# Attention steps in four rounds instead of three, fenced loads, and one expert piece a round before the gate

## The chip, the cores and the metric

The kernel runs on one core of a Trainium2 chip, as one program. Its time is the device time of that core in microseconds (us): the median of several executions. TensorE (PE) does the matrix products, VectorE (DVE), ScalarE (ACT) and GpSimd (POOL) work on the elements, SyncE (SP) issues nearly all the loads and stores. Each engine goes through its own list of instructions in the order in which the program was written; an instruction waits until its operands are there and its buffer is free, and all that stands behind it on that engine waits with it.

## The reference

Banded attention over 4 batches, 8 heads, 576 positions and 64 columns a head, then a mixture of 4 experts over the 2304 rows that come out:

```python
scores = q @ k.T / 8                           # per head, 576 x 576
mask   = rel in [0, 32)                        # heads 0 to 3
         rel in [0, 128) and rel % 4 == 0      # heads 4 to 7
attn   = softmax(where(mask, scores, -1e9))
x      = (attn @ v) as (2304, 512)
p      = probs / (probs.sum(-1) + 1e-9)        # (2304, 4)
out    = sum over e of p[:, e] * (relu(x @ w1[e]) @ w2[e])    # 512 -> 1024 -> 512
```

## The kernel before

**Attention.** The positions of heads 4 to 7 are sorted by their remainder by 4, so that every head has a plain band of 32 positions. A *group* is one batch, one pair of heads and a third (192) of the positions; a *step* is two groups, and there are 24 steps. A step goes through eight stages: `s_qk` (48 small products into two PSUM banks, tiles `sc`), `s_max` (DVE adds the mask and takes the smallest value of the negated scores: `sm`, `nm`), `s_sub` (POOL), `s_exp` (ACT), `s_sum` (DVE: sum, plus 1e-9, reciprocal), `s_norm` (POOL), `s_tr` (PE transposes into one bank, tile `pt`, ACT copies it to `pts`) and `s_av` (PE: 48 small products with `v` into two banks, tiles `po`, ACT copies them into the rows of x, tile `xr`). The pool `pa` of these banks has four, handed out in turn.

**Rounds.** The main loop (L746) runs over rounds `n`. In a round each stage is issued for the step that is `lag` rounds old, in the order of the table `stages` (L374): scores, maximum, subtraction and exponential of the newest step, sum and normalization of the one before, the transpose of the one two rounds back, `s_av` of the one three back. After step 4 and after step 9 three rounds start no step (`GAP`), so that the first positions of a batch are finished before the next are begun. All loads are issued by SP from `load_scores` and `load_values`, ahead of the stages and in one queue with the weights (`fetch_w1`, `fetch_w2`).

**Experts.** Each expert is cut into 4 *units* of 256 hidden columns: 16 units, each gone through twice (first for the 768 rows of block 0, then for blocks 1 and 2). Every fp32 operand is split into a high and a low part (ACT writes the high one, DVE or POOL the low one), and a product is three products of parts. x @ w1 of a unit is done with seven half-size products and sums of operands (Strassen-like): `x_sums` (L206, DVE) makes the sums of x in place, in tile `xr`, four a call; `x_part` (L218) splits one; `w1_split`, `w1_sums`, `w1_late` do the same for w1. Unit 0 of block 0 uses eight plain products instead (`plain`). The generator `experts` (L516 ff.) yields after each *piece*: 6 products of 384 columns (m1x, m1y) or one row tile of the second layer (6 products of 512 columns, tile `m`, which DVE adds to `acc`). A later visit of a unit has 13 pieces.

**How the two are interleaved.** Before round START (7) the rounds hold attention alone and dummy products (`dummies`, tile `wt`). From START on a round also takes pieces, 2 until round OPEN (15), where the *gate* opens, and `PACE` (10) from there on. Before the gate there are 7 pieces to do, the first half of unit 0; when they are done a round gets 6 dummies instead. With each piece `step()` runs one stage of a queue of splits and sums. After the last round, `gate` gets "over", and from the next time that a visit calls `begin()` the attention's pools are closed, larger ones are opened, and the parts of x of block 2 (`x_part` 4 and 5, `x_sums` 4 and 5) are queued. In the visit of unit 14 `need(x_sums, 5)` runs whatever of them is left at once.

The change touches the stage table, the eps addition in `s_sum`, the loads, the counts of pieces and dummies, and where unit 1's weights are split.

Of the kernel before, what the change touches and what calls it, by code (L numbers as in the profile page):

```python
# [21 lines left out]
PACE = 10  # L22
LAG = 3
# [3 lines left out]
FILL = 6  # L27
# [23 lines left out]
def kernel(  # L51
# [34 lines left out]
    ident = const.tile([128, 128], F32, name="ident")  # L86
    pw = const.tile([128, NTT, E], F32, name="pw")
# [39 lines left out]
    def w1_split(u):  # L127

        r = raw1[u]
        gh = wp.tile([128, 3, 2, 128], F32R, tag="g1h", name="g1h", bufs=2)  # L130
        gl = wp.tile([128, 3, 2, 128], F32R, tag="g1l", name="g1l", bufs=2)
        a11, a12 = r[:, 0:2, 0:128], r[:, 2:4, 0:128]
        a21, a22 = r[:, 0:2, 128:256], r[:, 2:4, 128:256]
        for i, a in enumerate((a11, a12, a22)):
            split(gh[:, i], gl[:, i], a, nc.scalar, nc.gpsimd if u > 1 else nc.vector)
            a_op[u, ("A11", "A12", "A22")[i]] = (gh[:, i], gl[:, i])
            yield
        if u == 0:
            gh, gl = (wp.tile([128, 4, FU], F32R, tag=t, name=t) for t in ("g2h", "g2l"))
            v = (slice(None), slice(0, 2), slice(128, 256))  # L140
            split(gh[v], gl[v], a21, nc.scalar, nc.vector)
            a_op[u, "A21"] = (gh[v], gl[v])
# [16 lines left out]
    def w1_late(u):  # L159
        r = raw1.pop(u)  # L160
        gh = wp.tile([128, 4, FU], F32R, tag="g2h", name="g2h")
        gl = wp.tile([128, 4, FU], F32R, tag="g2l", name="g2l")
        for n, c, f in (("S2", 0, 0), ("S1", 2, 128), ("S3", 0, 128), ("S4", 2, 0)):
            v = (slice(None), slice(c, c + 2), slice(f, f + 128))
            split(gh[v], gl[v], r[v], nc.scalar, nc.gpsimd if u > 1 else nc.vector)
            a_op[u, n] = (gh[v], gl[v])
            yield
        if u + 2 <= LAST:
            fetch_w1(u + 2)
# [59 lines left out]
    def attention(ap, xrp, pa):  # L229
# [78 lines left out]
        def s_sum(n, gs):  # L308
# [4 lines left out]
            nc.vector.tensor_scalar(  # L313
                out=su, in0=su, scalar1=1e-9, scalar2=None, op0=ALU.add
# [59 lines left out]
        stages = (  # L374
            (s_qk, 0), (s_av, 3), (s_tr, 2), (s_max, 0), (s_sum, 1), (s_sub, 0),
            (s_norm, 1), (s_exp, 0),
        )
        return chunk, load_masks, load_qk, load_v, stages
# [124 lines left out]
    def experts(begin):  # L503

        for half in range(2):
# [5 lines left out]
            if half == 1:  # L511
# [5 lines left out]
                prepare(w1_late, 1, soon=True)  # L517
# [76 lines left out]
    with tc.manual_schedule():  # L594
        make_identity(nc, ident)
        warm = ident.bitcast(mybir.dt.bfloat16)
# [30 lines left out]
        def done(*gs):  # L627

            return LAG + max(at(n) for n, s in enumerate(steps) if any(g in s for g in gs))

# [4 lines left out]
        def at(n):  # L635

            return n + GAP * sum(n > last for last in needed)

# [106 lines left out]
        first = 2 * (needed[0] + 1)  # L745
        dummies(18)  # L746
        ffn = experts(begin)
        for n in range(at(len(steps) - 1) + LAG + 1):
            load_scores(first if n <= needed[0] else len(flat))
            load_values(min(n + 1, qk_done // 2 + 3))  # L750
            for stage, lag in stages:
                m = step_at.get(n - lag)
                if m is not None:
                    stage(m, steps[m])
            if n in step_at:
                qk_done += 2
            av_done += n - LAG in step_at
# [17 lines left out]
            if n == 6:  # L775
                fetch_w1(1)
            if n == START:
                weigh(shares)
            if n == START + 1:
                prepare(w1_split, 1)  # L780
                prepare(w1_sums, 1)
            if n == OPEN - 1:
                prepare(w2_late, 1)
            if n == START + 2:
                fetch_w2(1)
            if n == OPEN:
                fetch_w1(2)
            if n == OPEN:
                gate.add("open")
            if n < START:  # L790
                dummies(FILL if n in step_at else FILL // 2)
# [5 lines left out]
            for _ in range(PACE if "open" in gate else 2):  # L797
                if next(ffn) == "idle":
                    dummies(FILL)
                    for _ in range(3):  # L800
                        step()
                    break
# [66 lines left out]
```

## Time and profile before

| | |
|---|---|
| median of 3 runs | 866.12 us (863.88 to 866.41) |
| the profiled execution | 863.98 us, of which the span of the trace is 862.2 us |
| PE busy | 825.6 us (96%), 6214 products |
| PE weight loads (PEld) | 730.6 us (85%) |
| DVE, ACT, POOL busy | 497.5 (58%), 320.4 (37%), 391.1 us (45%) |
| DMA | 59.18 MB, mean 69 GB/s |

Busy times are unions of the instructions' durations; products overlap one another in the array, so a PE busy to 100% is not the same in every stretch. "Idle before, releaser" in a row is the time in which the engine stood still before that instruction, and what ended it. PEclk is the share of the full TensorE clock that was granted (1.00 is 2.4 GHz, 0.50 is 1.2 GHz, values between them are means). The first 64 us are the rounds before the gate, then rounds and pieces run together until about 310 us, and the rest is experts alone.

### The profile page before, as it was taken

Reading aid. Unit: us, or ns where it says so; the run is one execution under the profiler, and the core shown is the slowest. Engines: PE = TensorE matmul, PEld = TensorE weight load, DVE = VectorE, ACT = ScalarE, POOL = GpSimd, SP = SyncE. Lnnn points to the kernel's source line nnn. Section 1 sums busy time; section 2 is a strip of 40 time slices with the busy share of each in tenths; the row PEclk is TensorE's granted clock in tenths of the full one; section 3 lists DMA queues with packets and bytes.
Section 4 is the critical chain, followed back from the end, with each engine's and each line's share of the span. In section 5 each row is a group of like instructions: output and inputs, shape, how many; then the busy total and the mean of one; then the engine's idle time right before and its main releaser. Section 6 shows DMA issues by size and latency. Waiting matters only on the chain.

```text
span 862.2 us, 15616 instructions
## 1 busy us (share of the span) xinstructions
PE 825.6 (96%) x6214; PEld 730.6 (85%) x6214; DVE 497.5 (58%) x1051; ACT 320.4 (37%) x759; POOL 391.1 (45%) x466
## 2 busy tenths in 40 slices
PE   7788999999989997899999999999999999999998
PEld 5657888889878896888989989899898898998986
DVE  4586667656865558655555555555545555555454
ACT  2454445445553444532422323333233242232321
POOL 3252768867767668633413422431432342342210
PEclk9899999999999999899999999999999999999999
DMA  7952323443422121301010010100100101000003
GB/s 218 232 142 92 107 85 97 127 138 101 126 69 75 67 74 50 123 24 49 25 49 25 27 49 25 49 25 25 50 25 24 49 25 48 26 25 25 0 24 123
DMA packets 49172, 59.18 MB, mean 69 GB/s; under 512 B 3641, under 2 KB 38585, under 8 KB 49099
## 3 DMA queue, kind: packets, MB, share of 16 engines
q1 hardware_dynamic: 48379, 57.53, 21.6%
q8 instruction: 49, 0.80, 0.4%
q10 hardware_dynamic: 720, 0.66, 0.2%
q14 instruction: 24, 0.20, 0.1%
HBM read 53.45 MB, written 4.72 MB: 67 GB/s over the span
## 4 chain that ended last, share of the span: by engine, by line
PE 86%; DVE 6%; DMA 2%; ACT 2%; POOL 1%; issue 1%; SPq 1%; ACTq 0%; DVEq 0%; POOLq 0%
PE m L483 44%; PE m1x L385 22%; PE m1y L385 17%; DVE xr L212 1%; PE po L352 1%; PE pt L332 1%; DMA v_s<-vw 1%; DVE acc L491 1%; PE sc L271 1%; DMA r<-w 1%; DVE sm L285 1%; SPq L256 1%; DVE xl_B L125 1%; DVE hl L409 1%; DVE xl_T L125 1%
## 5 line engine op out<-in xcount | busy, mean ns | idle before, releaser
L491 DVE SCALAR_TENSOR_TENSOR acc<-m,pn,acc 128x512 f32<-128x512 f32 x270 | 201.9, 749 | 136.3 <-PE m L483 135.9
L483 PE MATMUL m<-w2h,hh 128*128 128x512 f32 x576 | 228.0, 396 | 4.3 <-ACT hh L403 3.9
L483 PE MATMUL m<-w2l,hh 128*128 128x512 f32 x576 | 226.4, 393 | 0.0
L125 POOL TENSOR_TENSOR g2l<-r,g2h 128x256 fp32r<-128x256 f32 x120 | 88.7, 767 | 239.8 <-PE m L483 213.4
L483 PE MATMUL m<-w2h,hl 128*128 128x512 f32 x576 | 179.3, 393 | 0.0
L403 ACT ACTIVATE hh<-s 128x384 fp32r<-128x384 f32 x94 | 49.4, 526 | 248.0 <-DVE s L426 189.8
L483 PEld LDWEIGHTS m<-w2h,hh 128*128 128x128 f32 x576 | 108.8, 189 | 26.4 <-ACT hh L403 4.8
L483 PEld LDWEIGHTS m<-w2h,hl 128*128 128x128 f32 x576 | 108.7, 189 | 23.9
L483 PEld LDWEIGHTS m<-w2l,hh 128*128 128x128 f32 x576 | 108.9, 189 | 20.1
L125 POOL TENSOR_TENSOR w2l<-r,w2h 128x512 fp32r<-128x512 f32 x60 | 77.4, 1312 | 43.3 <-ACT w2h L122 43.1
L125 POOL TENSOR_TENSOR g1l<-r,g1h 128x256 fp32r<-128x256 f32 x90 | 67.2, 759 | 65.1 <-ACT g1h L122 65.1
L442 DVE TENSOR_TENSOR s<-m1x,s 128x384 f32<-128x384 f32 x47 | 26.2, 558 | 106.9 <-PE m1x L385 99.8
L435 ACT ACTIVATE u<-m1x 128x384 f32<-128x384 f32 x47 | 23.1, 491 | 143.3 <-PE m1x L385 143.2
L409 DVE SCALAR_TENSOR_TENSOR hl<-s,hh 128x384 fp32r<-128x384 f32 x94 | 58.0, 616 | 28.3 <-ACT hh L403 28.1
L385 PE MATMUL m1x<-xh_T,g2h 128*128 128x384 f32 x156 | 52.8, 338 | 1.9 <-DVE s L426 1.4
L385 PE MATMUL m1x<-xh_T,g2l 128*128 128x384 f32 x156 | 52.5, 336 | 0.6 <-POOL g2l L125 0.6
L385 PE MATMUL m1x<-xl_T,g2h 128*128 128x384 f32 x156 | 52.5, 337 | 0.0
L385 PE MATMUL m1y<-xh_B,g2h 128*128 128x384 f32 x128 | 43.4, 339 | 2.0 <-ACT s L439 2.0
L122 ACT ACTIVATE g2h<-r 128x256 fp32r<-128x256 f32 x125 | 43.7, 405 | 0.8 <-POOL r L154 0.7
L385 PE MATMUL m1y<-xl_B,g2h 128*128 128x384 f32 x128 | 43.2, 338 | 0.0
L385 PE MATMUL m1y<-xh_B,g2l 128*128 128x384 f32 x128 | 43.1, 336 | 0.0
L385 PE MATMUL m1x<-xh_T,g1h 128*128 128x384 f32 x96 | 33.2, 346 | 8.7 <-DVE s L442 7.7
(98 smaller groups left out, 1500.5 us busy)
## 6 DMA issues: line engine op xcount, KB each, us to landing
r<-w SPq DMA_DIRECT2D x64, 512.0 KB, 3.5
v_s<-vw SPq DMA_DIRECT2D x48, 192.0 KB, 4.1
k_s<-kT SPq DMA_DIRECT2D x44, 112.0 KB, 3.4
q_s<-qT SPq DMA_DIRECT2D x48, 96.0 KB, 3.3
out<-acc SPq DMA_DIRECT2D x18, 256.0 KB, 2.0
k_s<-kT ACTq DMA_DIRECT2D x4, 112.0 KB, 3.3
mask<-masks ACTq DMA_DIRECT2D x1, 192.0 KB, 3.1
pt__426<-probs SPq DMA_DIRECT2D x1, 36.0 KB
```

What stands on the lines that cost most here:

```text
L122: nc.scalar.activation(out=hi, in_=src, func=AF.Copy)
L125: lo_eng.tensor_tensor(out=lo, in0=src, in1=hi.bitcast(F32), op=ALU.subtract)
L212: nc.vector.tensor_tensor(out=quarter(i, d), in0=quarter(i, a), in1=quarter(i, b), op=ALU.subtract)
L256: nc.sync.dma_start(out=t[KB * k:KB * (k + 1)], in_=vw[b, p][:, :, gi * GB:(gi + 1) * GB, :])
L271: nc.tensor.matmul(banks[swap][o:o + QB, i * KB:(i + 1) * KB], q_s[h, c0:c0 + QB], k_s[h, c0:c0 + KB], start=True, stop=True, skip_group_c ...
L385: nc.tensor.matmul(bank, w[:, k], x[:, k], start=(first and k == 0 and i == 0), stop=(last and k == 1 and i == 2), skip_group_check=True,)
L403: nc.scalar.activation(out=hi, in_=src, func=AF.Relu)
L409: nc.vector.scalar_tensor_tensor(out=lo, in0=src, scalar=0.0, in1=hi.bitcast(F32), op0=ALU.max, op1=ALU.subtract)
L435: nc.scalar.activation(out=u2, in_=x, func=AF.Copy)
L442: nc.vector.tensor_tensor(out=s5, in0=x, in1=s5, op=ALU.add)
L483: nc.tensor.matmul(po, h, w, start=(n == 0 and x == 0), stop=(n == 3))
L491: nc.vector.scalar_tensor_tensor(out=acc, in0=po, scalar=pn[:, tt, e:e + 1], in1=acc, op0=ALU.mult, op1=ALU.add,)
```

## The change

- **Stages.** Steps 0 to 9 keep the old table (`first`). Steps from 10 on (`then`) have the subtraction and the exponential one round after the scores, the sum and normalization two after, the transpose three and `s_av` four after; and in a round the new step's scores and maximum come last instead of first. `lag` is 3 or 4 accordingly, and one more round is run at the end.
- **Loads.** Within the loop over `needed` (steps 4 and 9) the loads of later steps are held back until all the scores and values up to that step have been issued. `fetch_w1(1)` moves from round 6 to round 4, ahead of the loads of steps 5 to 9, and `fetch_w2(1)` from round 9 to round 8.
- **Pieces.** One a round before the gate, whether or not it is a round with a step; 3 calls of `step()` in each; six dummies in each round where no piece is left and in each round before START. After the gate 11 pieces a round with a step and 4 in one without.
- **Weights of unit 1.** All its splits and sums are queued at START, `w2_late` of it 3 rounds later; unit 0's last part goes into the tiles `u2` and `s5`, so that `g2h` and `g2l` are free for unit 1; what is left of `w1_late(1)` runs at round 16, and `fetch_w1(3)` behind it.
- **Eps.** The 1e-9 of `s_sum` is added from a tile by `tensor_tensor` instead of `tensor_scalar`.

```diff
-PACE = 10
-LAG = 3
+PACE = 11
...
-            gh, gl = (wp.tile([128, 4, FU], F32R, tag=t, name=t) for t in ("g2h", "g2l"))
-            v = (slice(None), slice(0, 2), slice(128, 256))
-            split(gh[v], gl[v], a21, nc.scalar, nc.vector)
-            a_op[u, "A21"] = (gh[v], gl[v])
+            ah, al = (
+                fp.tile([128, TH], F32R, tag=t, name=t)[:, :FU].rearrange("p (c f) -> p c f", c=2)
+                for t in ("u2", "s5")
+            )
+            split(ah, al, a21, nc.scalar, nc.vector)
+            a_op[u, "A21"] = (ah, al)
...
-        if u + 2 <= LAST:
+        if 1 < u and u + 2 <= LAST:
             fetch_w1(u + 2)
...
-            nc.vector.tensor_scalar(
-                out=su, in0=su, scalar1=1e-9, scalar2=None, op0=ALU.add
+            nc.vector.tensor_tensor(
+                out=su, in0=su, in1=eps.to_broadcast([128, 2 * GS]), op=ALU.add
             )
...
-        stages = (
+        first = (
             (s_qk, 0), (s_av, 3), (s_tr, 2), (s_max, 0), (s_sum, 1), (s_sub, 0),
             (s_norm, 1), (s_exp, 0),
         )
+        then = (
+            (s_sub, 1), (s_sum, 2), (s_av, 4), (s_tr, 3), (s_norm, 2), (s_exp, 1),
+            (s_qk, 0), (s_max, 0),
+        )
+        stages = (first, then)
...
-                prepare(w1_late, 1, soon=True)
...
-        first = 2 * (needed[0] + 1)
         dummies(18)
         ffn = experts(begin)
-        for n in range(at(len(steps) - 1) + LAG + 1):
-            load_scores(first if n <= needed[0] else len(flat))
-            load_values(min(n + 1, qk_done // 2 + 3))
-            for stage, lag in stages:
-                m = step_at.get(n - lag)
-                if m is not None:
-                    stage(m, steps[m])
+        for n in range(at(len(steps) - 1) + 5):
+            ahead = qk_done // 2 + (3 if n > needed[0] else 1)
+            for last in needed:
+                load_scores(2 * last + 2)
+                load_values(min(last + 1, ahead))
+                if v_next <= last:
+                    break
+                if last == needed[0] and n == last:
+                    fetch_w1(1)
+            else:
+                load_scores(len(flat))
+                load_values(ahead)
+            for k, order in enumerate(stages):
+                for stage, after in order:
+                    m = step_at.get(n - after, -1)
+                    if m >= 0 and k == (m > needed[1]):
+                        stage(m, steps[m])
+                        av_done += stage == order[(1, 2)[k]][0]
...
-            if n == 6:
-                fetch_w1(1)
             if n == START:
                 weigh(shares)
-            if n == START + 1:
                 prepare(w1_split, 1)
                 prepare(w1_sums, 1)
-            if n == OPEN - 1:
+                prepare(w1_late, 1)
+            if n == START + 1:
+                fetch_w2(1)
+            if n == START + 3:
                 prepare(w2_late, 1)
-            if n == START + 2:
-                fetch_w2(1)
             if n == OPEN:
                 fetch_w1(2)
+            if n == OPEN + 1:
+                need(w1_late, 1)
+                fetch_w1(3)
...
-                dummies(FILL if n in step_at else FILL // 2)
+                dummies(FILL)
...
-            for _ in range(PACE if "open" in gate else 2):
+            if "open" not in gate:
                 if next(ffn) == "idle":
                     dummies(FILL)
-                    for _ in range(3):
-                        step()
-                    break
+                for _ in range(3):
+                    step()
+                continue
+            for _ in range(PACE if n in step_at else 4):
+                next(ffn)
                 step()
```

Three places show how the instructions stand now. The first is PE in a round behind the gate, at the point where a round's attention work meets the pieces; `sc`, `po`, `pt` are the banks of scores, of attention times v, and of the transpose. Before:

```order
L385 MATMUL m1x<-xl_T_0_1047,g1h 128x384
L271 MATMUL sc<-k_s,q_s 32x64 x24
L352 MATMUL po<-pts,v_s 64x32 x24
L332 MATMUL pt<-ident,sm 128x128 x3
L385 MATMUL m1y<-xh_B_0_712,g1h 128x384
```

The same place in the changed kernel:

```order
L490 MATMUL m_2025<-w2h,hl 128x512 x2
L354 MATMUL po<-pts,v_s 64x32 x24
L334 MATMUL pt<-ident,sm 128x128 x3
L273 MATMUL sc<-k_s,q_s 32x64 x24
L392 MATMUL m1x<-xh_T_0_1201,g2h 128x384
```

The scores went from the first place to the last. With five banks a round out of four, it was the transpose that got the bank that the same round's scores had held; now it is the second bank of scores that gets the one that the same round's first `po` held.

The second is SP's queue of loads before the gate: `r1` is a unit's w1, `r2` its w2, `v_s` the values of a step, and two rows each of `q_s` and `k_s` its scores' operands. Before, from the last load for the scores of step 7 on:

```order
L250 DMA k_s_552<-kT 128x224
L256 DMA v_s_555<-vw 64x2x384 x2
L256 DMA v_s_614<-vw 64x2x384 x2
L107 DMA r1_651<-w1 128x4x256
L256 DMA v_s_671<-vw 64x2x384 x2
L249 DMA q_s_796<-qT 128x192
L250 DMA k_s_797<-kT 128x224
L249 DMA q_s_800<-qT 128x192
L250 DMA k_s_801<-kT 128x224
L256 DMA v_s_804<-vw 64x2x384 x2
L115 DMA r2_849<-w2 128x2x512
```

In the changed kernel unit 1's w1 stands further ahead, right behind the values of step 4 and in front of the scores of step 5:

```order
L258 DMA v_s_442<-vw 64x2x384 x2
L107 DMA r1_445<-w1 128x4x256
L251 DMA q_s_447<-qT 128x192
L252 DMA k_s_448<-kT 128x224
L251 DMA q_s_451<-qT 128x192
```

and behind the scores of step 7 follow the values of steps 5 to 7, unit 1's w2 and step 8:

```order
L252 DMA k_s_556<-kT 128x224
L258 DMA v_s_559<-vw 64x2x384 x2
L258 DMA v_s_624<-vw 64x2x384 x2
L258 DMA v_s_685<-vw 64x2x384 x2
L115 DMA r2_786<-w2 128x2x512
L251 DMA q_s_797<-qT 128x192
L252 DMA k_s_798<-kT 128x224
L251 DMA q_s_801<-qT 128x192
L252 DMA k_s_802<-kT 128x224
L258 DMA v_s_805<-vw 64x2x384 x2
```

So w1 moved ahead of the scores of steps 5 to 7, and w2 ahead of the scores and values of step 8.

The third is DVE where block 2's x is prepared, in the visit of unit 14: `xr<-xr` are the sums of `x_sums`, `acc` the additions of the second layer, `hl` and `u`, `s` the work on the first layer's results. Before:

```order
L125 TENSOR_TENSOR xl_B_2_4765<-xr,xh_B_2_4764 128x2x192
L212 TENSOR_TENSOR xr<-xr 128x2x192 x8
L491 SCALAR_TENSOR_TENSOR acc_851<-m_4778,pn,acc_851 128x512
L491 SCALAR_TENSOR_TENSOR acc_851<-m_4790,pn,acc_851 128x512
L491 SCALAR_TENSOR_TENSOR acc_851<-m_4804,pn,acc_851 128x512
L442 TENSOR_TENSOR s_4815<-m1x,s_4815 128x384
```

In the changed kernel:

```order
L214 TENSOR_TENSOR xr<-xr 128x2x192
L453 TENSOR_TENSOR u_4614<-m1y,u_4614 128x384
L416 SCALAR_TENSOR_TENSOR hl<-s_4615,hh 128x384
L416 SCALAR_TENSOR_TENSOR hl<-u_4614,hh 128x384
L214 TENSOR_TENSOR xr<-xr 128x2x192
L416 SCALAR_TENSOR_TENSOR hl<-m1x,hh 128x384
L214 TENSOR_TENSOR xr<-xr 128x2x192 x2
L498 SCALAR_TENSOR_TENSOR acc_1017<-m_4690,pn,acc_1017 128x512
L214 TENSOR_TENSOR xr<-xr 128x2x192
L498 SCALAR_TENSOR_TENSOR acc_1017<-m_4703,pn,acc_1017 128x512
L214 TENSOR_TENSOR xr<-xr 128x2x192
L498 SCALAR_TENSOR_TENSOR acc_1017<-m_4714,pn,acc_1017 128x512
```

The eight sums stood in one block before; now six of them are spread over the rows shown, and the last two stand behind them, on both sides of the next `s` and `hl`. With the new counts the last round ends just before the visit of unit 13 calls `begin()`; before, it ended six pieces behind that call. So the pools are closed one visit earlier, and between the closing and `need(x_sums, 5)` lie 14 pieces where there was one.

## Rows read from the trace of the kernel before

**Rows 1.** Busy time of each engine in three stretches, PEclk, DMA share, GB/s

```profile
core 0: us, PE busy (x) PEld busy (x) DVE busy (x) ACT busy (x) POOL busy (x), PEclk, DMA share, GB/s
20.00:40.00 20.00, 15.04 (x291) 11.93 (x289) 9.69 (x33) 9.04 (x26) 5.02 (x6) 0.84 0.94 235
340.00:360.00 20.00, 12.87 (x50) 11.45 (x51) 14.53 (x22) 7.81 (x19) 12.78 (x14) 0.74 0.21 67
380.00:400.00 20.00, 20.00 (x103) 18.25 (x103) 10.84 (x18) 8.53 (x20) 9.59 (x13) 1.00 0.08 27
```

**Rows 2.** PE in time before the gate: start us, us, instruction [idle, releaser]

```profile
18.00 1.47 PE L352 MATMUL po<-pts,v_s 64*64 64x32 f32 x48
39.96 0.80 PE L483 MATMUL m<-w2h,hh 128*128 128x512 f32 x1 [3.28 <-ACT hh L403]
44.53 0.97 PE L271 MATMUL sc<-k_s,q_s 64*32 64x64 f32 x48
...
51.91 0.72 PE L271 MATMUL sc<-k_s,q_s 64*32 64x64 f32 x48
...
63.28 0.45 PE L385 MATMUL m1x<-xh_T,g1h 128*128 128x384 f32 x1 [1.05 <-ACT xh_T L122]
```

**Rows 3.** The chain of waits, 19 to 91 us: start us, us, what

```profile
19.19 7.89 DMA v_s<-vw
...
32.05 7.04 DMA r<-w
...
39.96 4.65 PE m L483 x10
...
82.21 0.52 ACT sm L306
...
84.47 1.04 PE m1x L385 x6
...
86.55 4.12 PE m L483 x18
```

**Rows 4.** The page's DMA issues: name, queue, count, KB each, us to landing

```profile
r<-w SPq DMA_DIRECT2D x64, 512.0 KB, 3.5
v_s<-vw SPq DMA_DIRECT2D x48, 192.0 KB, 4.1
k_s<-kT SPq DMA_DIRECT2D x44, 112.0 KB, 3.4
q_s<-qT SPq DMA_DIRECT2D x48, 96.0 KB, 3.3
```

**Rows 5.** PE in time behind the gate

```profile
76.88 0.41 PE L385 MATMUL m1x<-xh_T,g2h 128*128 128x384 f32 x1 [1.41 <-DVE s L426]
...
83.16 0.44 PE L385 MATMUL m1y<-xh_B,g2h 128*128 128x384 f32 x1 [2.04 <-ACT s L439]
```

**Rows 6.** Who waited for whom: us in total, times, longest us

```profile
ACT sm L306 <- POOL sm L299: 25.1, 21, 5.1
...
PE pt L332 <- DVE nm L285: 5.9, 5, 1.4
```

**Rows 7.** PE in time, one round at 119 us

```profile
119.38 0.90 PE L352 MATMUL po<-pts,v_s 64*64 64x32 f32 x48
121.38 0.52 PE L332 MATMUL pt<-ident,sm 128*128 128x128 f32 x3 [1.10 <-DVE nm L285]
```

**Rows 8.** ACT in time, the same round

```profile
120.31 0.55 ACT L368 ACTIVATE xr<-po 128x192 f32<-128x192 f32 x2 [0.93 <-PE po L352]
```

**Rows 9.** PE in time, where block 2's x is prepared

```profile
347.13 0.69 PE L385 MATMUL m1x<-xh_T,g1h 128*128 128x384 f32 x1 [7.67 <-DVE s L442]
...
351.13 0.63 PE L483 MATMUL m<-w2h,hh 128*128 128x512 f32 x1
```

**Rows 10.** DVE in time, the same place

```profile
336.55 8.09 DVE L212 TENSOR_TENSOR xr<-xr 128x384 f32<-128x384 f32 x8
```

**Rows 11.** DVE groups: line, operation, count | busy us, mean ns | idle before

```profile
L212 DVE TENSOR_TENSOR xr<-xr 128x384 f32<-128x384 f32 x24 | 20.1, 842 | 0.5
...
L313 DVE TENSOR_SCALAR su<-su 128x6 f32<-128x6 f32 x24 | 10.9, 453 | 0.8
...
L125 DVE TENSOR_TENSOR xl_B<-xr,xh_B 128x384 fp32r<-128x384 f32 x11 | 9.8, 906 | 4.6 <-ACT xh_B L122 4.6
```

More of the change, by code (lines that the diff above doesn't have):

```diff
@@ L86 @@
     ident = const.tile([128, 128], F32, name="ident")
+    eps = const.tile([128, 1], F32, name="eps")
     pw = const.tile([128, NTT, E], F32, name="pw")
@@ L595 @@
         make_identity(nc, ident)
+        nc.gpsimd.memset(eps, 1e-9)
         warm = ident.bitcast(mybir.dt.bfloat16)
@@ L627, in done @@
         def done(*gs):
-            return LAG + max(at(n) for n, s in enumerate(steps) if any(g in s for g in gs))
+            return max(at(n) + lag(n) for n, s in enumerate(steps) if any(g in s for g in gs))
         needed = [
@@ L637, in at, with lag @@
             return n + GAP * sum(n > last for last in needed)
+        def lag(n):
+            return 3 if n <= needed[1] else 4
         step_at = {at(n): n for n in range(len(steps))}
@@ L743, in load_values @@
                 v_next += 1
-        first = 2 * (needed[0] + 1)
         dummies(18)
         ffn = experts(begin)
-        for n in range(at(len(steps) - 1) + LAG + 1):
-            load_scores(first if n <= needed[0] else len(flat))
-            load_values(min(n + 1, qk_done // 2 + 3))
-            for stage, lag in stages:
-                m = step_at.get(n - lag)
-                if m is not None:
-                    stage(m, steps[m])
+        for n in range(at(len(steps) - 1) + 5):
[16 more added lines that the diff above has]
+                        av_done += stage == order[(1, 2)[k]][0]
             if n in step_at:
                 qk_done += 2
-            av_done += n - LAG in step_at
             for i, names in when.get(n, ()):
```

## The prediction

> **What bounds the kernel now.** I read the busy times first. PE is busy for 825.6 of 862.2 us, so whatever a change does here, it does it by taking away idle time, half-clock time or dummies. The stretches [rows 1] say where these are. From 380 us on PE is busy all the time at the full clock, and such a stretch can give nothing. From 20 to 40 us PE lacks 5 us and the DMA engines are busy to 94%: loads set the pace. From 340 to 360 us PE lacks 7 us at a mean clock of 0.74, with DVE busier than anywhere else shown. So I went through PE in time for the gaps. Before the gate there is one of 3.28 us, whose releaser, followed back, is the landing of unit 1's w1, 7 us after its issue [rows 2, 3]; the pieces run again at 39.96, the scores of step 9 at 51.91, and the first piece behind the gate at 63.28. Behind the gate two gaps of 1.41 and 2.04 us [rows 5], then five of a transpose that waits for DVE, 5.9 us in all [rows 6], then one of 7.67 us [rows 9]. The reader should see that each has another engine at its end, so that they don't go together.
>
> The sum is made against the profiled execution, 863.98 us. It stands 2.1 us under the median of the runs, 866.12.
>
> **Up to the gate.** The pieces before the gate are the same seven in both kernels. What decides is when the scores of step 9 run, since from there to the first piece behind the gate the order on DVE, POOL and ACT is nearly the same: 63.28 - 51.91 = 11.4 us [rows 2]. The 3.28 us wait for w1 goes, since w1 is now asked for right behind the values of step 4, which land at 19.19 + 7.89 = 27.1 us [rows 3]. What is late next is the load of step 8. In KB [rows 4] a step's scores are 2 x (96 + 112) = 416, its values 2 x 192 = 384, a unit's w1 or w2 512. From 27.1 us to the scores of step 8 the queue now holds both weights, four steps' scores and three steps' values: 1024 + 1664 + 1152 = 3840 KB, 3.93 MB, and at 235 GB/s [rows 1] that is 16.7 us: they land at 43.8. The scores of step 9 come 800 KB later, at 47.3, and this end of the queue moves the same loads as before.
>
> PE has run out of work by then. By the same rate the scores of step 7 land at 34.8 us (1760 KB, 7.7 us); with them, a transpose and a piece PE is done at about 38, and stands until 43.8. A gap of 3.28 us was followed by slow products: ten took 4.65 us at 39.96, where 18 take 4.12 at the full clock [rows 3], which is the lower of the two levels, 1.2 GHz, against 2.4. I expect the same behind this longer gap. The round at 43.8 has scores, po, a transpose and a third of those 18: at the full clock 0.72 + 0.90 + 0.52 + 1.37 = 3.5 us [rows 2, 7], at half 0.97 + 1.47 [rows 2] + 0.85 (the transpose in po's ratio) + 6 x 0.465 = 6.1 us. So the scores of step 9 run between 47.3 and 49.9 us instead of 51.91. I take 49.6, near the slow end because the gap is the longer one: a gain of 2.3 us, between 2.0 and 4.6 while the loads come at this rate, and nothing or a loss if they don't (a rival below). The rounds behind it have pieces of 1.37 us where they had six dummies; both lie beside the softmax of step 9, which is what is waited for.
>
> The eps addition takes 453 ns as a tensor_scalar [rows 11]. As a tensor_tensor of 6 columns no row shows it; it saves between nothing and 0.45, on a path of two steps at most 0.9 us. I take nothing. Dummies: 78 instead of 90, none of them where something waits for PE; nothing.
>
> **Behind the gate.** At 83.16 PE waits for ACT's copy of s [rows 5], and just ahead of this copy ACT ran the exponential of step 10 [rows 3], which had waited for POOL. Now step 10's exponential is a round later, and unit 1's weights, which were split in front of it, are ready: the 2.04 us go. The 1.41 at 76.88 has splits of unit 1 and of x before it on DVE; the first are gone, the second stay: half, 0.7. Together 2.7, between 1 and 3.5.
>
> **In the rounds.** The five waits of the transpose for DVE, 5.9 us [rows 6], go: its bank is now one that was read a round ago. In their place the second bank of scores waits for ACT to copy the first po of the same round, in ten rounds. Rows of one round price it: po ends at 119.38 + 0.90 = 120.28, ACT starts at 120.31 and needs half of 0.55 for the first copy [rows 7, 8], to 120.6; PE has the transposes meanwhile, 0.52 us, begun while po drains. That leaves 0 to 0.3; I take 0.25, 2.5 us in ten rounds. Where ACT is behind with a piece's work it costs more: as price I take 0.8, in two rounds, since the old wait had 1.0 to 1.4 in five. Together 4.1 instead of 5.9: a gain of 1.8 us, between 5.9 (ACT always in time) and a loss of 8.1 (1.4 in all ten).
>
> **Block 2's sums.** Eight sums in a row hold DVE for 8.09 us [rows 10], and behind them stands the addition that PE waits for: 7.67 us idle. Then PE starts at half clock: two pieces of the first layer take 351.13 - 347.13 = 4.0 us [rows 9] instead of 2 x 1.04 [rows 3], 1.9 more. Now the sums stand one by one between other work, over nine pieces of the second layer and eight of the first: 9 x 1.37 + 8 x 1.04 = 20.7 us of PE. DVE's own work is 10.84 us in 20 [rows 1], 11.2 in this stretch. The sums take 0.84 on the mean and 1.01 in the block, three splits of x 0.91 [rows 10, 11]: 11.2 + 8.1 + 2.7 = 22.0 us, 1.3 more than PE needs. I leave that 1.3 as a wait: 7.67 + 1.9 - 1.3 = 8.3 us gained, between 2.5 (a rival) and 9.6.
>
> The Trainium skill speaks against spreading them: "SBUF — State Buffer", in "Who interferes with whom", says that a VectorE instruction with two SBUF inputs contends with GpSimd's reads for one shared pair of ports, held for a whole instruction. By it a sum would be slow wherever POOL works, and the sum above would be kept by 1.01 us a sum, as it is, and not by the mean.
>
> **Sum.** 2.3 + 2.7 + 1.8 + 8.3 = 15.1; 863.98 - 15.1 = 848.9 us. The median may stand up to 2 us above a profiled execution, as it does before; I forecast 849.5.
>
> **The rivals.**
> - The sums still hold PE up, one at a time. For it: seven places with a single or double sum now stand in front of an s, hl or acc that PE or ACT waits for, and each sum takes up to 1.01 us [rows 10]. Against: DVE has slack of 9 us in 20 [rows 1], and after the closing four banks of the second layer lie between PE and DVE. 7 x 1.01 = 7.1 instead of 1.3: 855.3 us. The skill's rule above would be its cause. Chance 0.13.
> - The gate opens no earlier. For it: both kernels move the same bytes up to the scores of step 9, and the idle time before step 8 is longer than the one it replaces. Against: in the kernel before, step 9's scores ran 4.6 us behind the time that the rate gives. The 2.3 us are lost, and up to 3 more at half clock: 851.8 to 854.8. Chance 0.11.
> - The earlier closing doesn't do what it says: the new pools' tiles lie where attention's lay, and the last round is now only a piece or so old. Then PE waits there instead, for as long as before: 849.5 + 8.3 = 857.8. Against: the last copies of po need some 0.5 us [rows 8], and attention's other buffers were read earlier still. Chance 0.08.
> - The slower side: ACT becomes what each round waits for. The exponential now stands right behind the copies that PE needs and in front of all of a piece's work on ACT, and it waits for POOL's subtraction: 25.1 us in 21 times, up to 5.1 [rows 6]. If a round's scores or the next piece then lose p each in ten rounds, the forecast has p = 0.41; at p = 1.8 nothing is gained, and from p = 2.4 on it is slower: 849.5 + 10 x 2.0 = 869.5. Against: the mean of these waits is 1.2, PE hardly shows them today, and the subtraction no longer waits for the maximum of its own round. Chance 0.08, of which 0.05 slower.
>
> **How the numbers follow.** The forecast has 0.60: its own range, from the bounds above, is 843 to 853. Within 0.3% (2.6 us, about what a measurement of this kernel can tell from no change) lies 863.5 to 868.7. The first three rivals are faster too, which makes 0.92 for faster, 0.03 for no change, 0.05 for slower. The range of 842 to 858 leaves out the slower side and the case that all gains reach their upper bounds (4.6 + 3.5 + 5.9 + 9.6 = 23.6: 840.4).
>
> **What would show it.** Right: no gap of several us around 330 to 345 and a clock of 1.00 there, with single sums on DVE; a gap of about 6 us before the scores of step 8, at 38 to 44; the first piece behind the gate at about 61; no wait of a transpose for DVE from step 10 on, and short ones of scores for ACT's xr copies. Wrong: the first piece behind the gate at 63 or later, gaps of 1 us or more at the scores in most rounds, or a gap of several us near the closing of the pools. The forecast fails as a whole if PE's gaps behind the gate add up to more than 12 us.

## The result and the profile after

The changed kernel takes 845.55 us (844.84 to 845.76, 4 runs) against 865.7 us for the kernel before: ratio 0.977, 95% interval 0.975 to 0.979. The forecast was 849.5, its range 842 to 858. The profiled execution has 844.84 us (span 843.1), 19.1 less than the one before.

The stretches of [rows 1], and the one behind the first, in the kernel after (same columns):

```profile
20.00:40.00 20.00, 14.09 (x336) 11.16 (x335) 14.85 (x60) 10.51 (x28) 6.38 (x8) 0.92 0.91 247
40.00:60.00 20.00, 17.40 (x377) 13.37 (x375) 13.55 (x58) 10.56 (x28) 10.85 (x12) 0.74 0.63 175
320.00:340.00 20.00, 20.00 (x100) 17.94 (x99) 17.23 (x26) 9.71 (x24) 17.68 (x19) 1.00 0.24 80
340.00:360.00 20.00, 20.00 (x101) 17.98 (x101) 13.32 (x19) 7.80 (x19) 14.82 (x16) 1.00 0.41 132
```

PE stands still nowhere between 320 and 360 us. Before the gate it still does, and from 40 to 60 us runs at a mean clock of 0.74. PE in time up to the gate, against [rows 2]:

```profile
38.48 0.90 PE L334 MATMUL pt<-ident,sm 128*128 128x128 f32 x3 [4.04 <-POOL sm L323]
...
42.37 0.92 PE L273 MATMUL sc<-k_s,q_s 64*32 64x64 f32 x44 [0.62 <-DMA k_s<-kT]
...
48.33 0.97 PE L273 MATMUL sc<-k_s,q_s 64*32 64x64 f32 x48
...
60.23 0.44 PE L392 MATMUL m1x<-xh_T,g1h 128*128 128x384 f32 x1 [1.05 <-ACT xh_T L122]
```

Step 8's scores run at 42.4 us (43.8 predicted), those of step 9 at 48.33 (49.6), the first piece behind the gate at 60.23 (61) instead of 63.28. One sign of the prediction did not come: the long idle time ahead of step 8 is not one of about 6 us that ends with its load. It is 4.04 us, ahead of the transpose at 38.48, which waits for POOL's normalization (`sm`); the load of step 8 then holds PE up for 0.62.

Behind the gate PE's gaps of 0.15 us or more are these and one of 0.62 us at 241 us, against [rows 5, 6, 9]:

```profile
72.72 0.45 PE L392 MATMUL m1x<-xh_T,g2h 128*128 128x384 f32 x1 [0.72 <-DVE s L433]
...
161.28 0.50 PE L490 MATMUL m<-w2h,hh 128*128 128x512 f32 x1 [1.40 <-DVE acc L498]
...
247.16 0.50 PE L490 MATMUL m<-w2h,hh 128*128 128x512 f32 x1 [0.78 <-DVE acc L498]
252.26 0.69 PE L273 MATMUL sc<-k_s,q_s 64*32 64x64 f32 x44 [0.84 <-ACT xr L370]
...
315.90 0.44 PE L392 MATMUL m1x<-xh_T,g1h 128*128 128x384 f32 x1 [0.49 <-DVE s L449]
```

Together 4.85 us; before they were 19.6. The 2.04 us of [rows 5], the five waits of the transpose and the 7.67 us are gone. DVE where block 2's sums now stand, against [rows 10]:

```profile
318.61 1.10 DVE L214 TENSOR_TENSOR xr<-xr 128x384 f32<-128x384 f32 x1
...
320.09 1.64 DVE L214 TENSOR_TENSOR xr<-xr 128x384 f32<-128x384 f32 x2
...
323.89 0.99 DVE L214 TENSOR_TENSOR xr<-xr 128x384 f32<-128x384 f32 x1
324.80 0.74 DVE L498 SCALAR_TENSOR_TENSOR acc<-m,pn,acc 128x512 f32<-128x512 f32 x1
325.46 0.54 DVE L214 TENSOR_TENSOR xr<-xr 128x384 f32<-128x384 f32 x1
...
328.56 2.06 DVE L498 SCALAR_TENSOR_TENSOR acc<-m,pn,acc 128x512 f32<-128x512 f32 x3
```

DVE falls behind, so that three additions stand together at the end, and PE doesn't notice: the pool `m2` that it writes the second layer into has four banks by then.

### The profile page after: what moved, and what is told of

It is laid out like the page before. It is cut to its first block, busy times and chain, and to the rows that moved or that the text cites. A ratio compares the mean times of both kernels' runs of the same rounds, so it can differ in the third digit from the quotient of the medians.

```text
span 843.1 us, 15570 instructions
## 1 busy us (share of the span) xinstructions
PE 821.0 (97%) x6196; PEld 726.3 (86%) x6196; DVE 490.1 (58%) x1051; ACT 320.6 (38%) x759; POOL 391.6 (46%) x467
## 4 chain that ended last, share of the span: by engine, by line
PE 90%; DVE 4%; POOL 3%; ACT 1%; DMA 1%; issue 1%; POOLq 0%; SPq 0%; DVEq 0%; ACTq 0%
PE m L490 45%; PE m1x L392 23%; PE m1y L392 17%; PE po L354 2%; PE sc L273 1%; DMA v_s<-vw 1%; PE pt L334 1%; PE wt L716 1%; DVE xr L214 1%; DVE sm L287 1%; POOL sm L301 0%; DVE acc L498 0%; POOL xl_B L125 0%; DVE hl L416 0%; POOL xl_T L125 0%
## 5 line engine op out<-in xcount | busy, mean ns | idle before, releaser
L122 ACT ACTIVATE w2h<-r 128x512 fp32r<-128x512 f32 x64 | 38.3, 621 | 0.0
```

The source lines that it names most:

```text
L122: nc.scalar.activation(out=hi, in_=src, func=AF.Copy)
```

## The experiments

My theory: four terms that don't depend on one another, of which the largest (block 2's sums) comes from the earlier closing alone. Each run below takes out or puts in one of them.

### Block 2's sums: closed late, in a block, and the counts alone

Closed late, on the changed kernel:

```diff
             if "over" in gate and "m1" not in gate:
+                if "late" not in gate:
+                    gate.add("late")
+                    return
                 gate.add("m1")
```

> The changed kernel, but the attention's pools are closed at the second call of begin() after the last round (194 pieces done) instead of the first (181), as it was before; rounds, loads, table and unit 1 stay changed. Theory (the sums' term comes from the earlier closing alone): the parts and sums of block 2 stand in one block again, PE waits 7 to 8 us for DVE at about 330 us and starts again at half clock; 845.6 + 9.6 = 855, between 853 and 857. Rival (the rounds' new order or the shorter rest of attention removed that wait, the closing did not): 845 to 848, and no gap over 2 us there.

Sums in a block, on the changed kernel:

```diff
                     assert "m1" in gate
+                    for i in (4, 5):
+                        prepare(x_sums, i, of=later)
                     need(x_sums, 5)
...
-                for i in (4, 5):
-                    prepare(x_sums, i, of=later)
```

> The changed kernel, closing at 181 pieces, but the eight sums of x_sums 4 and 5 are held back and issued in one block at need(x_sums, 5); the six splits of B11, B21 and B22 stay spread. Theory: the block of sums itself (8.09 us of DVE in the kernel before) is what PE waited for; four banks of the second layer (4 x 1.37 = 5.5 us of PE) hide part of it, so a gap of 3 to 8 us with half clock behind it: 849 to 855. Rival (the six splits that stood in front of the sums made the difference, or the earlier and larger second-layer pool): under 847.5 and no gap over 2 us at about 330 us.

The counts alone, on the kernel before:

```diff
-PACE = 10
+PACE = 11
...
-            for _ in range(PACE if "open" in gate else 2):
+            for _ in range((PACE if n in step_at else 4) if "open" in gate else 2):
```

> The kernel before with one edit: 11 pieces a round with a step and 4 in a round without one behind the gate, so that attention ends at piece 177 and the pools close at 181 instead of 194. Old table, old loads, unit 1 as before. Theory: the term of block 2's sums alone, 865.7 - 9.6 = 856, between 854.5 and 858, with no gap over 2 us between 325 and 355 us. Rival (11 pieces a round need the new table, since the transposes' waits for DVE grow with it): 859 to 864, with more than 5.9 us of waits of the transpose for DVE.

Measured: 855.02 closed late (ratio to before 0.988, 0.987 to 0.990), 851.36 in a block (0.985, 0.982 to 0.987), 852.23 with the counts alone (0.986, 0.983 to 0.988). PE and DVE closed late:

```profile
339.22 0.69 PE L392 MATMUL m1x<-xh_T,g1h 128*128 128x384 f32 x1 [7.65 <-DVE s L449]
```

```profile
328.64 8.08 DVE L214 TENSOR_TENSOR xr<-xr 128x384 f32<-128x384 f32 x8
```

The old gap is back to 0.02 us, in a kernel whose rounds, loads and table are new. With the sums in a block, but closed early:

```profile
336.56 0.44 PE L392 MATMUL m1x<-xh_T,g1h 128*128 128x384 f32 x1 [4.08 <-DVE s L449]
```

The block of sums alone makes 5.8 us of the 9.5. The other 3.7 go with the six splits that had to run in front of it in the old place, or with the larger banks coming later; these two I did not part. And the counts alone, in the kernel before, leave this of the gap:

```profile
320.74 0.44 PE L385 MATMUL m1x<-xh_T,g1h 128*128 128x384 f32 x1 [0.51 <-DVE s L442]
```

But they gain 12.7 us (13.0 by the profiles), more than the 8 to 11 expected. Part of the surplus has a place: PE behind the gate has the 1.41 us wait, and no longer the 2.04 us one at 83 us. Another 0.76 us lie ahead of the gate, which this edit doesn't touch: the first piece behind it stands at 62.52 instead of 63.28. By so much the gate moves from one execution to the next.

```profile
76.12 0.41 PE L385 MATMUL m1x<-xh_T,g2h 128*128 128x384 f32 x1 [1.41 <-DVE s L426]
...
78.92 0.45 PE L385 MATMUL m1x<-xh_T,g2h 128*128 128x384 f32 x1 [0.25 <-ACT u L435]
...
140.53 0.50 PE L483 MATMUL m<-w2h,hh 128*128 128x512 f32 x1 [0.84 <-DVE acc L491]
```

### The table: taken out, and alone

```diff
-        stages = (first, then)
+        stages = (first, first)
...
-            return 3 if n <= needed[1] else 4
+            return 3
...
```

> The changed kernel with the old stage table and a lag of 3 for all steps; piece counts, closing, loads and unit 1 stay changed. Theory (the table is worth the transposes' waits less the new waits, 3.2 us by the traces): 845.6 + 3.2 = 848.8, between 847.5 and 850, with 5 to 7 us of waits of the transpose for DVE. Rival A (the fourth round also takes the softmax out of the way of the pieces on ACT and DVE, and carries part of what I ascribe to unit 1 behind the gate): 851 to 854, with a wait at the first pieces behind the gate again. Rival B (PE's waits in the rounds only change their place): 845 to 846.5.

The other way round, on the kernel before: the new table and lag, no pieces in the added round.

```diff
...
-            for _ in range(PACE if "open" in gate else 2):
+            for _ in range((PACE if n < 33 else 0) if "open" in gate else 2):
```

> The kernel before with the new stage table and lag of 4 from step 10 on alone; the added last round gets no pieces, so that attention still ends at piece 187 and the pools close at 194. Prediction's reading: the five waits of the transpose for DVE (5.9 us) go and scores wait for ACT here and there instead, and step 10's exponential stands a round later, so that the 2.04 us wait behind the gate goes too: 864.9 - 5.9 - 2.0 + 1.5 = 858.5, between 857 and 861. Rival (from the run with the old table in the changed kernel, where it cost 1.2 us only: which wait a round shows depends on where the pieces fall, and 10 pieces a round give other waits for those removed): 863 to 865, with over 4 us of other waits in the rounds.

Measured: without the table 846.73 (ratio to before 0.979, 0.977 to 0.982), so 1.2 more than the changed kernel, or 2.1 by the ratios, with overlapping intervals: less than the 3.2 expected, and not clear of no difference. Its transposes wait for DVE for 2.7 us behind the gate, not 5 to 7. The table alone takes 861.68 (0.996, 0.994 to 0.997), 3.9 less than before and 3.5 by the profiles. By PE's gaps it should have been more: from the gate to 100 us they fall from 4.45 to 2.41 us (the 2.04 goes here too), from 100 to 312 us from 6.83 to 3.40. That makes 5.5 us, and its gate, which the table doesn't touch, opens another 0.9 earlier (62.40); 2.9 of this are given back, in no gap. PE in one round of the kernel before, from the first small product to the next piece:

```profile
192.60 0.72 PE L271 MATMUL sc<-k_s,q_s 64*32 64x64 f32 x48
193.26 0.90 PE L352 MATMUL po<-pts,v_s 64*64 64x32 f32 x48
194.14 0.52 PE L332 MATMUL pt<-ident,sm 128*128 128x128 f32 x3
194.41 0.42 PE L385 MATMUL m1y<-xh_B,g2h 128*128 128x384 f32 x1
```

And in the changed kernel:

```profile
201.70 0.90 PE L354 MATMUL po<-pts,v_s 64*64 64x32 f32 x48
202.54 0.55 PE L334 MATMUL pt<-ident,sm 128*128 128x128 f32 x3
203.01 0.72 PE L273 MATMUL sc<-k_s,q_s 64*32 64x64 f32 x48
203.66 0.45 PE L392 MATMUL m1y<-xh_B,g2h 128*128 128x384 f32 x1
```

194.41 - 192.60 = 1.81 us against 203.66 - 201.70 = 1.96, with no wait in either. A transpose and a piece have one shape of tile (128\*128); where the piece came right behind it, it started 0.27 us later, and where the scores (64\*32) come behind it, 0.47. In the rounds without a wait it is 1.79 to 1.91 against 1.96 or 1.97. Over all small products of the rounds behind the gate it makes 1.7 us (27.1 against 25.5), ten rounds of the new order having all three kinds. The Trainium skill has the rule, in "TensorEngine Tiling (Array Packing)", "Key Properties": a change of tiling mode drains TensorE. These rows agree with it: the old order has three changes of shape a round, the new one four. That the fourth change is what costs the 0.15 us is my reading of the rows; no run varies the number of changes alone.

### The loads alone

On the kernel before: the block of loads with its fences as in the change, `fetch_w1(1)` behind the values of step 4, `fetch_w2(1)` at round 8; nothing else.

```diff
-            load_scores(first if n <= needed[0] else len(flat))
-            load_values(min(n + 1, qk_done // 2 + 3))
+            ahead = qk_done // 2 + (3 if n > needed[0] else 1)
+            for last in needed:
+                load_scores(2 * last + 2)
+                load_values(min(last + 1, ahead))
...
```

> The kernel before with the changed kernel's order of loads alone (unit 1's w1 behind the values of step 4, its w2 a round earlier, the fences). Pieces two a round before the gate, counts, table and splits as before. Theory: the 3.28 us wait for w1 goes, the scores of step 9 run at 48 to 50.5 us instead of 51.91, and the first piece behind the gate stands at 60 to 62 instead of 63.28; nothing changes behind it: 864.9 - 2.5 = 862.4, between 861 and 864. Rival (one piece a round instead of two is what lets the gate open earlier, since the softmax of steps 7 to 9 then shares DVE and ACT with less): first piece at 63 or later, 864.5 to 866.

Measured: 862.53 (ratio 0.997, 0.996 to 0.999), 3.1 less by the medians. The scores of step 9 ran at 49.84 us; PE behind them:

```profile
61.22 0.44 PE L385 MATMUL m1x<-xh_T,g1h 128*128 128x384 f32 x1 [1.05 <-ACT xh_T L122]
...
74.82 0.41 PE L385 MATMUL m1x<-xh_T,g2h 128*128 128x384 f32 x1 [1.41 <-DVE s L426]
...
81.10 0.69 PE L385 MATMUL m1y<-xh_B,g2h 128*128 128x384 f32 x1 [2.03 <-ACT s L439]
```

The gate opens 2.1 us earlier, and behind it both old waits stand. One piece a round instead of two is not needed for it. By the profiles the whole is only 1.2 us: in this execution the clock fell to 0.50 behind the 2.03 us wait (82 to 84 us), where the kernel before had 1.00, and by 121 us 1.5 us are lost again.

### Unit 1's weights as before

On the changed kernel:

```diff
...
             if n == START:
                 weigh(shares)
+            if n == START + 1:
                 prepare(w1_split, 1)
                 prepare(w1_sums, 1)
-                prepare(w1_late, 1)
-            if n == START + 1:
                 fetch_w2(1)
-            if n == START + 3:
+            if n == OPEN - 1:
                 prepare(w2_late, 1)
...
```

> The changed kernel with unit 1's splits and sums queued when they were before (a round later, its last part only behind the gate, w2's split at the round before the gate, the fetch of unit 3's w1 behind that part); counts, table, loads stay changed. Theory by the prediction: the waits of 1.41 us and part of the 2.04 us behind the gate come back, 845.6 + 2.7 = 848.3, between 847 and 849.5. Rival (the 2.04 us went with the counts, as in the run with the counts alone, and only 0.7 to 1.1 us of the first wait hang on unit 1): 846 to 847, a gap of about 1.4 us near 73 us and none over 1 us from 75 to 90 us.

Measured: 847.99 (0.981, 0.978 to 0.983), 2.4 more. PE, and the windows behind the gate:

```profile
60.70 0.44 PE L392 MATMUL m1x<-xh_T,g1h 128*128 128x384 f32 x1 [1.05 <-ACT xh_T L122]
...
61.73 0.53 PE L392 MATMUL m1x<-xl_T,g1h 128*128 128x384 f32 x1 [0.42 <-DVE xl_T L125]
...
75.89 0.41 PE L392 MATMUL m1x<-xh_T,g2h 128*128 128x384 f32 x1 [1.40 <-DVE s L433]
```

```profile
60.00:64.00 4.00, 2.89 (x10) 2.57 (x11) 3.73 (x6) 1.05 (x4) 0.66 (x1) 0.74 0.37 129
64.00:68.00 4.00, 4.00 (x64) 3.66 (x62) 1.05 (x3) 1.04 (x3) 0.00 (x0) 0.83 0.85 236
```

The 1.41 us is back (0.72 in the changed kernel) and the 2.04 us is not: the waits cost 1.35 us (1.40 + 0.42 + 0.25 - 0.72), of which the 0.7 that I had predicted for the 1.41. Another 1.6 us are clock: from 60.70 to 75.89 less the waits are 13.4 us, in the changed kernel from 60.23 to 72.72 11.8, at 1.00.

### PE's idle time before the gate, filled

```diff
+                    if n == START + 3 and stage == s_tr:
+                        dummies(32)
...
+                if n == START + 3:
+                    dummies(16)
```

(`s_tr` stands for its entry in the table.)

> The changed kernel with 32 dummies ahead of the transpose in round 10 and 16 behind that round's piece, which fill PE's idle time between 34.4 and 42.4 us. Theory (half clock after the idle time costs the rounds of steps 8 and 9 some 2.5 us; step 9's scores wait for PE and not for their load, which lands at 44.5): the granted clock from 40 to 60 us rises from 0.74 to above 0.95, the scores of step 9 run at 45.5 to 46.5 instead of 48.33, the first piece behind the gate at 57.5 to 58.5 instead of 60.23: 845.6 - 2.3 = 843.3, between 842.5 and 844.5. Rival (softmax of steps 8 and 9 on DVE, POOL and ACT sets the gate, whose engines do not change their clock): clock up, first piece at 59.5 to 60.5, 845 to 846.

The edit put the 32 in once for each of the two tables, 64 in all, and a dummy took 0.165 us; PE was held up by 10 us, and the run took 852.43 us (0.985, 0.981 to 0.988). Its scores of steps 8 and 9 stood 3.35 us apart (52.16, 55.51) instead of 5.96, at the full clock, which I took for the price of half clock. Four more runs follow. The first fills the idle time in the right measure:

```diff
+                    if n == START + 3 and k == 0 and stage == s_tr:
+                        dummies(20)
...
+                if n == START + 3:
+                    dummies(10)
```

> The changed kernel with 20 dummies ahead of round 10's transpose and 10 behind its piece: the idle time from 34.4 to 42.4 us filled in the right measure (a dummy took 0.165 us in the run with too many, where from the scores of step 8 to those of step 9 passed 3.35 us at the full clock instead of 5.96). Theory (half clock behind the idle time costs 2.6 us): the scores of step 9 at 45.5 to 46.5 instead of 48.33, the first piece behind the gate at 57.3 to 58.5 instead of 60.23, 845.6 - 2.4 = 843.2, between 842.3 and 844.6. Rival (the softmax of steps 6 to 9 on DVE, POOL and ACT sets the gate, whatever PE's clock): clock up from 40 to 60 us, first piece at 59.5 to 60.5, 845 to 846.

The next has the 20 but not the 10, and w2 later:

```diff
-            if n == START + 1:
-                fetch_w2(1)
             if n == START + 3:
+                fetch_w2(1)
+            if n == START + 6:
                 prepare(w2_late, 1)
```

> The changed kernel with the 20 dummies ahead of round 10's transpose, and with unit 1's w2 fetched two rounds later (behind the scores of step 9 instead of ahead of those of step 8; its split starts three rounds later). Theory (the load of step 8 is what PE waits for at 42.4 us): by 512 KB at 235 GB/s, 2.2 us, the scores of step 8 come earlier, at 40 to 40.5; those of step 9 at 44 to 45, the first piece behind the gate at 56.3 to 57.3; 842.2, between 841.2 and 843.5. Rival (step 6's normalization, whose POOL work ended at 42.8 us, now holds the transpose of that round): step 9's scores at 45.5 to 46.5, no better than with the dummies alone, 843 to 844.5.

And the third, as the second, with

```diff
-                for _ in range(3):
+                for _ in range({12: 1, 13: 4, 14: 4}.get(n, 3)):
                     step()
```

> As the one with dummies and the later w2, and one queued split or sum in round 12 instead of three, four in rounds 13 and 14, so that two of the three sums of x that stood on DVE in front of step 9's softmax sum (53.22 to 55.02 us) go behind it. Theory (step 9's softmax is on the chain to the gate: its transpose waited 0.90 us for POOL): another 0.9 us, 841.3, between 840.3 and 843. Rival (the first pieces behind the gate then wait for these sums and the split that follows them): no gain or up to 1 us lost, 842 to 844.5, with a gap of 0.5 to 2 us at the first pieces.

The fourth is the changed kernel once more.

> The changed kernel unchanged, as the measure for the three others on the same chip. 845.6, between 844.8 and 846.5; a difference of under 0.8 us between two of these kernels is not told apart.

Measured on one chip: 844.74 filled (ratio 0.976, 0.974 to 0.978), 846.44 with the later w2 (0.977, 0.975 to 0.980), 846.56 with fewer steps as well (0.979, 0.976 to 0.981), 844.19 the changed kernel again (0.975, 0.973 to 0.978). None beats it. PE with the idle time filled:

```profile
39.72 0.55 PE L334 MATMUL pt<-ident,sm 128*128 128x128 f32 x3 [0.86 <-POOL sm L323]
...
42.78 1.10 PE L273 MATMUL sc<-k_s,q_s 64*32 64x64 f32 x48
...
46.21 0.52 PE L334 MATMUL pt<-ident,sm 128*128 128x128 f32 x3 [1.50 <-DVE nm L287]
...
49.13 0.97 PE L273 MATMUL sc<-k_s,q_s 64*32 64x64 f32 x48
```

The clock was 1.00 from 40 to 46 us, and from scores to scores it took 6.35 us, no less than at half clock. What the dummies saved PE spent standing still: 1.50 us ahead of the transpose at 46.21, for DVE. Behind that wait the clock was 0.50 again (48 to 50 us), so the piece in front of step 9's scores ran slowly after all. The changed kernel run again has much the same without any dummy. Its window from 44 to 46 us, and that of its first execution:

```profile
44.00:46.00 2.00, 0.41 (x14) 0.33 (x7) 2.00 (x16) 0.85 (x3) 0.00 (x0) 1.00 0.19 31
```

```profile
44.00:46.00 2.00, 1.76 (x32) 1.63 (x29) 1.97 (x15) 0.67 (x3) 0.57 (x1) 0.50 0.02 5
```

PE at half clock is busy for 1.76 us; at the full clock it is done early and stands still for the bank that DVE's maximum of step 8 has to read first (1.59 us, against 0.24). Step 9's scores come at 48.63 and 48.33. DVE in the first execution:

```profile
42.56 0.56 DVE L416 SCALAR_TENSOR_TENSOR hl<-m1y,hh 128x384 fp32r<-128x384 f32 x1 [0.72 <-ACT hh L410]
43.04 0.75 DVE L125 TENSOR_TENSOR g2l<-r,g2h 128x256 fp32r<-128x256 f32 x2
43.71 0.68 DVE L125 TENSOR_TENSOR w2l<-r,w2h 128x512 fp32r<-128x512 f32 x1
44.31 0.22 DVE L287 CUSTOM_DVE_ANT_0 sm<-sc,mask 128x64 f32<-128x64 f32 x1
```

Step 8's scores are there at 43.3, and their maximum starts at 44.31, behind three splits, and these behind a copy of ACT that waited for the exponential of step 7. How long this chain of softmax and splits is can be read from DVE's maximum of step 6 to that of step 9. In the changed kernel's first execution, its second, the run filled, and the run with the loads alone (columns of [rows 1]):

```profile
35.26:49.73 14.47, 10.37 (x182) 8.20 (x184) 10.88 (x56) 6.35 (x16) 6.90 (x8) 0.55 0.73 212
```

```profile
36.01:50.48 14.47, 9.42 (x210) 7.30 (x210) 11.34 (x57) 6.31 (x16) 6.88 (x8) 0.76 0.74 204
```

```profile
36.50:50.98 14.48, 11.97 (x235) 8.33 (x233) 11.35 (x57) 6.31 (x16) 6.89 (x8) 0.88 0.81 224
```

```profile
39.21:50.68 11.47, 9.38 (x236) 6.39 (x237) 11.00 (x55) 3.72 (x9) 4.61 (x6) 1.00 0.47 130
```

The chain takes 14.47 or 14.48 us at a mean clock of 0.55, 0.76 and 0.88. The runs closed late and without the table, which are the same kernel up to the gate, have 14.47 too, at 0.54 and 0.65; only the run with the sums in a block has 15.02, since its step 8 was held up by its load until 43.42. So the rival's cause holds: the softmax and the splits on DVE, POOL and ACT set the gate, not PE's clock. With the idle time filled the gate stands later (61.27) because step 6 does. In the first run with dummies DVE had 10 us more to catch up; that, I take it, made the 3.35 us.

The last row shows what the change does to this chain. With the loads alone it is 11.47 us long and begins at 39.21; in the changed kernel it begins 4 us earlier (35.26), but unit 1's splits and the pieces now fall into it, and most of the head start is lost again. With unit 1's splits as before it is 12.82 us long, from 37.59 on. In all these runs the first piece behind the gate stands between 60.04 and 61.27 us.

With the later w2 step 8's scores came at 41.4 and the first piece behind the gate at 59.96, but then the clock fell where PE is what all wait for:

```profile
60.00:64.00 4.00, 3.57 (x13) 3.26 (x14) 3.00 (x6) 0.32 (x1) 0.00 (x0) 0.70 0.56 190
64.00:68.00 4.00, 4.00 (x64) 3.57 (x63) 1.81 (x8) 1.80 (x5) 0.00 (x0) 0.88 0.97 286
```

The piece that ran at 72.72 in the changed kernel stood at 74.44. Why the clock falls behind the gate in this run, in the third and in the one with unit 1's old splits, and not in the changed kernel, with nearly the same gaps in front, stays open.

## Why the prediction was right

**The gate** (2.3 predicted). 3.05 us by the first execution, 2.5 by the second, 2.1 with the loads alone. Kernels that are the same up to the gate have its first piece at 62.40, 62.52 and 63.28 us (the old one) and between 60.04 and 61.18 (five executions of the new one); the means lie 2.2 us apart. So the term holds, and so does its source, the order of loads. The path to the number was in part another; that the number came out so near is luck to this extent. The load of step 8 came about when the prediction has it (42.4 us), but PE had stood still for POOL, and waited 0.62 us for it instead of 6. And "I expect the same behind this longer gap", that half clock sets the time from step 8's scores to those of step 9, gave 6.1 us and came to 5.96, but with the full clock from 44 to 46 us (the second execution) and from 40 to 46 us (with dummies) it is 6.1 and 6.4 as well. What sets it is the chain of softmax and splits, 14.47 us at mean clocks from 0.54 to 0.88. From step 9's scores to the gate 11.9 us passed, not 11.4.

**Behind the gate** (2.7). The waits there fall by 3.7 us. Of the 1.41, half went, as worked out. Another 1.0 went that the prediction didn't have: 0.42 us at 64.32 for DVE's `xl_T` and 0.58 at 68.98 for ACT's `hh`, both in the kernel before. The 2.04 went, but not for one reason: the new counts alone remove it (old table, old splits) and so does the new table alone (old counts). What is common is that step 10's exponential no longer stands just ahead of that copy; unit 1's splits were not needed for it, and whether they alone would do it was not run.

**In the rounds** (1.8). The waits fall by 3.2 us (6.83 to 3.64), more than predicted: the 0.25 that I took for the second bank of scores in each round was 0, and a wait of that kind came once, with 0.84. A cost that the prediction didn't have takes 1.7 of it back, the fourth change of shape a round. Net 1.5 (1.2 by the run without the table, 2.1 by its ratio): the term was near by two errors that cancel. And the new counts by themselves had already cut the transposes' waits for DVE behind the gate from 5.9 us to 2.7, though all waits in the rounds together only from 6.83 to 6.30.

**Block 2's sums** (8.3). 9.5 us by the run closed late. By the rows it is a gap of 7.67 and a neighbour's of 0.63, less the 0.49 that remains, and 1.7 (closed late) to 2.5 us (before) of half clock. The mis-sized term is the 1.3 us that DVE would be behind: it was behind, but four banks took it. On the Trainium skill's rule weighed there ("SBUF — State Buffer", "Who interferes with whom") the rows agree: the one sum that falls in POOL's pause (325.46; POOL works to 325.48 and again from 327.41) took 0.54 us, the singles beside POOL's work 0.88 to 1.10. That the rival built on it came to nothing is, I take it, the banks' doing; no run has fewer of them.

**Eps and dummies**: the addition takes 351 ns on the mean instead of 453 [rows 11], 0.52 us on the path to the gate (at 45.75); nothing, as taken. The traces have 66 dummies instead of 84, where the prediction has 78 and 90; nothing hangs on them.

```profile
L315 DVE TENSOR_TENSOR su<-su,eps 128x6 f32<-128x6 f32 x24 | 8.4, 351 | 0.9
```

**The sum.** By the rows 3.05 + 3.7 + 1.5 + 10.3 = 18.6 of the 19.1 us. Another 1.0 comes evenly behind 370 us, where no engine's order differs: the 97th addition to `acc` stands 18.1 us earlier than before, the last 19.1. The runs without the table and with the late closing have this too, the three on the old kernel (counts, table, loads) don't. Its cause is open, as are the 0.5 us by which the sum is too large.

## What to carry to other kernels

A block of work that must be done "by then" costs what stands in front of the waiting instruction at that point; it pays to count where that point falls. Here the last round ended at piece 181, just ahead of a `begin()`, instead of at 187, and this was worth more than all that was done to the order of stages. In this case half clock was a cost only where PE was what all waited for: look whether the product behind the slow stretch waited for another engine anyway before filling the idle time. And when the order of small products is changed, count the changes of tile shape, since they leave no gap to be seen.

## What I had not expected of the hardware

Transposes (128\*128) followed by products of 64\*32 cost PE 0.15 us a round more than the same transposes followed by 128\*128 products, with PE shown as busy throughout. And two executions of one kernel ran the same stretch at a granted clock of 0.50 and of 1.00 (44 to 46 us), and the softmax chain around it took 14.47 us in both.
